# Gathering expert tokens before the last spectral tile: an early indirect gather, a one-hot product in PSUM, and transposes moved ahead

## The chip, the cores and the metric

The kernel runs on one core of a Trainium2 chip. The metric is the device time of one execution in microseconds (us). Before the change it is 496.32 us, the median of three runs (497.5, 496.32 and 492.94). Beside them stands one profiled execution of 498.16 us, whose span from first to last instruction is 496.4 us. All times of single instructions below come from that execution, and positions such as "at 401.55" are us from the start of its span.

## The reference, cut to what matters

Two blocks follow each other. The first filters each of 8 sequences (2496 positions, 256 channels) in the frequency domain. The second is a mixture of 8 experts: each token goes to the expert with the largest gate logit, each expert keeps the 80 tokens with the largest gate weight, and all other output rows are zero.

```python
X = np.fft.rfft(x, axis=1)
y = np.fft.irfft(X * (filt_r + 1j * filt_i)[None], n=2496, axis=1)   # (8, 2496, 256)
x = y.reshape(19968, 256)
logits = x @ w_gate
expert_idx = np.argmax(logits, axis=1)
gate_w = softmax(logits)[np.arange(N), expert_idx]
for e in range(8):
    tok_idx = np.where(expert_idx == e)[0]
    if len(tok_idx) > 80:
        tok_idx = the 80 of them with the largest gate_w
    h = np.maximum(x[tok_idx] @ w1[e], 0.0)            # w1[e]: 256 x 1024
    out[tok_idx] = gate_w[tok_idx, None] * (h @ w2[e])  # w2[e]: 1024 x 256
```

## The kernel before

Until about 300 us the kernel transforms all 8 sequences, writes their filtered spectra to DRAM (`yf`) and gets the gate logits directly from the spectra. Only then does it know which tokens are kept, and it transforms only those back. Kept tokens are grouped in 8 tiles of up to 128 tokens, one tile for each sequence.

**Choosing the tokens (`pick_...`, called from L871 on).** VectorE (DVE) and TensorE (PE) find the 80 best tokens of each expert. The last step, `pick_slots(2)` (L694), adds 16 small bf16 products in a PSUM tile called `misc` (L697), copies the result to `es` (L701) and derives from it three index tables: `idxg`, the row of `y_sel` that holds each token of each expert, `idxs`, its row in the output, and `idxt`, its row in the table of gate weights (`tokens`, L1048 to L1066). `es[:, 1]` is the tile of a token, `es[:, 0]` its place in the tile.

**Back transform of tile t.** `fetch(t)` (L467, a gather on the queue of GpSimd, POOL) brings rows of a table, `turn_rows(t, g)` (L483) transposes them on PE and ScalarE (ACT) copies them to SBUF, `add_rows(t, g)` (L493) adds 20 products of 128x256 in PSUM (L498). When a tile is complete, ACT copies it to `yr` (L502) and ACT's DMA queue writes it to `y_sel` in DRAM (L503). The order of the work on PE is the hand-written list `work` (L825 to L832), run piece by piece by `go`; the schedule is manual, so each engine executes in program order. Tiles come in order 0 to 7. On the way `spectrum(t)` (SyncE's queue, SP) loads spectra, and `weights(e, ...)` loads the 2 MB of each expert's weights on the SP queue: experts 0 and 1 after tile 4, 2 after tile 5, 3 to 5 when the buffers of the last spectra and table rows come free, 6 and 7 when experts 0 and 1 are done with theirs.

**Experts (class `Experts`, L995).** `gather(e)` (L1001) is an indirect DMA on the POOL queue which collects the 80 tokens of expert e from `y_sel`; since `y_sel` is read as a whole, it waits for the writes of all 8 tiles. `layer1(e)` (L1010) transposes the gathered rows on PE (L1015, 2 transposes), lets DVE copy them to `xs` (L1018), multiplies by w1 (L1022, 16 products of 128x80, which the profile lists as 32 records because an f32 product is two) and applies the ReLU, half on ACT (L1027), half on DVE (L1028). `layer2(e)` (L1032) multiplies by w2 (L1037, 8 products of 80x256), scales on ACT (L1040) and scatters 80 rows into the output through the POOL queue (L1042). The loop at L910 to L917 runs gather(e+3), layer1(e+1), layer2(e), after a first layer1(0) at L909. So each expert's transposes stand directly before its own products on PE.

Of the kernel before, what the change touches and what calls it, by code (L numbers as in the profile page):

```python
# [10 lines left out]
AL = mybir.AluOpType  # L11
AF = mybir.ActivationFunctionType
AX = mybir.AxisListType
F32 = mybir.dt.float32
BF16 = mybir.dt.bfloat16
# [8 lines left out]
B, S, C = 8, 2496, 256  # L24
# [57 lines left out]
def kernel(  # L82
# [95 lines left out]
    nc.gpsimd.memset(ones_bf[:], 1.0)  # L178


    NE, NY = 3, 2
    yf = {b: dpool.tile([128, NS, C], F32, name=f"yf_{b}") for b in range(B)}
    ypool = ctx.enter_context(tc.tile_pool(name="spec", bufs=NY))
    ysb = {}
# [48 lines left out]
    with ExitStack() as actx:  # L233
# [246 lines left out]
        def weights(e, p, tag):  # L480
            load_weights(e, p.tile([128, 2 * NFC * C], F32, name=f"w_{e}", tag=tag))
# [11 lines left out]
        def add_rows(t, g):  # L493
            if g == 0:
                pos[t] = yps.tile([128, 2, 512], F32, name=f"po_{t}", tag="y")
            for i in range(SG):
                s = SG * g + i
                nc.tensor.matmul(pos[t][:, 0, 0:C], lhsT=wts[t, g // 2][:, g % 2, i, :],  # L498
                                 rhs=ybs[t][:, s, :], start=(s == 0), stop=(s == NS - 1))
            if g == NS // SG - 1:  # L500
                yr = t2pool.tile([128, 2, C], F32, name=f"yr_{t}", tag="t2")
                nc.scalar.copy(out=yr[:, 0, :], in_=pos[t][:, 0, 0:C])  # L502
                nc.scalar.dma_start(out=y_sel[128 * t:128 * t + 128, :], in_=yr[:, 0, :])  # L503

        def pt(shape, dt, name, rnd):
# [168 lines left out]
        def pick_slots(part):  # L674
            f_t = st["f_t"]
            if part == 0:
                off_e = pt([128, 1], F32, "off_e", 1)
                nc.vector.tensor_copy(out=off_e[:], in_=st["poff"][:, 2, 0:1])
                slot = pt([128, KR], F32, "slot", 1)
                nc.vector.tensor_scalar(out=slot[:], in0=iota[:, 0:KR], scalar1=off_e[:, 0:1],  # L680
                                        scalar2=None, op0=AL.add)
                st["eplc"] = xpool.tile([128, KR, cap], BF16, name="eplc", tag="x")
                nc.vector.tensor_tensor(
                    out=st["eplc"][:], in0=slot[:].unsqueeze(2).to_broadcast([128, KR, cap]),
                    in1=iota[:, 0:cap].unsqueeze(1).to_broadcast([128, KR, cap]),
                    op=AL.is_equal)
            elif part == 1:
                st["eval"] = pt([128, KR, 4, E], BF16, "eval_", 1)
                for i in range(4):
                    nc.gpsimd.tensor_tensor(  # L690
                        out=st["eval"][:, :, i, :],
                        in0=f_t[:, i, :].unsqueeze(2).to_broadcast([128, KR, E]),
                        in1=ehot[:].unsqueeze(1).to_broadcast([128, KR, E]), op=AL.mult)
            else:  # L694
                pe = st["misc"][0:cap, 128:128 + 4 * E]
                for k in range(KR):
                    nc.tensor.matmul(pe, lhsT=st["eplc"][:, k, :],  # L697
                                     rhs=st["eval"][:, k].rearrange("p v e -> p (v e)"),
                                     start=(k == 0), stop=(k == KR - 1))
                es = pt([cap, 4, E], F32, "es", 1)  # L700
                nc.vector.tensor_copy(out=es[:].rearrange("p v e -> p (v e)"), in_=pe)  # L701
                nc.vector.scalar_tensor_tensor(out=idxg[:], in0=es[:, 1, :], scalar=128.0,
                                               in1=es[:, 0, :], op0=AL.mult, op1=AL.add)
                emp = pt([cap, E], F32, "emp", 1)
                nc.vector.tensor_scalar(out=emp[:], in0=es[:, 3, :], scalar1=st["off"][0:cap, 0:1],
                                        scalar2=float(N + S), op0=AL.is_le, op1=AL.mult)
                tokens(nc, sp, cap, es[:, 1, :], 0.0, es[:, 2, :], es[:, 3, :], -1.0, emp, idxs,
                       idxt)

        LATE, LEAD = 2, 2  # L710
        with tc.manual_schedule():
# [182 lines left out]
            for t in range(NE, 6):  # L894
                fetch(t)
            go(1)
            pick_slots(2)
            go(next(i for i, w in enumerate(work) if w[1] == NE))
            go(len(work))

            ex = Experts(nc, cap, ident, fp, lambda n: fps.tile([128, 512], F32, name=n, tag="f"),
                         lambda n: yps.tile([128, 2, 512], F32, name=n, tag="y"), y_sel[0:128 * B, :], out,
                         idxg, idxs, gate, w1s, w2s)
            for e in range(3):
                ex.gather(e)
            weights(3, st["yx"], "ys")
            weights(4, ypool, "ys")
            weights(5, t1pool, "t1")
            ex.layer1(0)  # L909
            for e in range(E):  # L910
                if e + 3 < E:
                    ex.gather(e + 3)
                if e + 1 < E:
                    ex.layer1(e + 1)
                ex.layer2(e)
                if e + 6 < E:
                    weights(e + 6, wpool, "w")  # L917

# [37 lines left out]
    with tc.If(n_bad > 0):  # L956
        with tc.tile_pool(name="spz", bufs=1) as mp:
            zc = mp.tile([128, C], F32, name="zc")
            nc.vector.memset(zc[:], 0.0)
            for t in range(B, B + NX):  # L960
                nc.sync.dma_start(out=y_sel[128 * t:128 * t + 128, :], in_=zc[:])
        select(tc, lg, cap, ident, ident_bf, iota, iota_i, pid, pid_i, lane, idxs, idxg, gate,
               idxb, more, nof, ohb)
        with (
            tc.tile_pool(name="xp2", bufs=1) as mp,
            tc.tile_pool(name="xps2", bufs=1, space=PSUM) as mps,
        ):
            for b in range(B):
                back(mp, mps, f"g{b}", lambda: spectrum_of(mp, b, f"g{b}"), 128 * b,
                     idxb[:, b:b + 1])  # L970
            for t in range(NX):
                ix = spill_lists(tc, mp, mps, t, cap, nof, ohb, iota, idxg)
                po = None
                for b in range(B):
                    po = back(mp, mps, f"x{t}_{b}", lambda: spectrum_of(mp, b, f"x{t}_{b}"),
                              128 * (B + t) if b == B - 1 else None, ix[:, b:b + 1],
                              start=(b == 0), stop=(b == B - 1), acc=po, pad=True)

        with (
            tc.tile_pool(name="w3", bufs=2) as wp3,  # L980
            tc.tile_pool(name="fp3", bufs=2) as fp3,
            tc.tile_pool(name="px3", bufs=2, space=PSUM) as px3,
            tc.tile_pool(name="ph3", bufs=2, space=PSUM) as ph3,
        ):
            ex = Experts(nc, cap, ident, fp3, lambda n: px3.tile([128, 512], F32, name=n, tag="f"),
                         lambda n: ph3.tile([128, 2, 512], F32, name=n, tag="y"), y_sel, out,
                         idxg, idxs, gate, w1s, w2s, "g")
            for e in range(E):
                load_weights(e, wp3.tile([128, 2 * NFC * C], F32, name=f"wg_{e}", tag="w"))
                ex.gather(e)  # L990
                ex.layer1(e)
                ex.layer2(e)


class Experts:  # L995
    def __init__(self, nc, cap, ident, fp, bank, banks, y_sel, out, idxg, idxs, gate, w1s, w2s,
                 nm=""):
        self.__dict__.update(locals())
        self.xg, self.hT = {}, {}

    def gather(self, e):  # L1001
        nc, cap = self.nc, self.cap
        xg = self.fp.tile([cap, C], F32, name=f"xg{self.nm}_{e}", tag="xg", bufs=4)
        nc.gpsimd.indirect_dma_start(
            out=xg[:], out_offset=None, in_=self.y_sel[:, :],
            in_offset=bass.IndirectOffsetOnAxis(ap=self.idxg[:, e:e + 1], axis=0),
            bounds_check=self.y_sel.shape[0] - 1, oob_is_err=False)
        self.xg[e] = xg

    def layer1(self, e):  # L1010
        nc, cap, nm = self.nc, self.cap, self.nm
        xg = self.xg.pop(e)
        px = self.bank(f"px{nm}_{e}").rearrange("p (k t) -> p k t", k=4)
        for k in range(NDB):
            nc.tensor.transpose(px[:, k, 0:cap], xg[:, 128 * k:128 * k + 128],  # L1015
                                self.ident[0:cap, 0:cap])
        xs = self.fp.tile([128, NDB, cap], F32, name=f"xs{nm}_{e}", tag="xs")
        nc.vector.tensor_copy(out=xs[:], in_=px[:, 0:NDB, 0:cap])  # L1018
        ph = self.banks(f"ph{nm}_{e}").rearrange("p i (j t) -> p i j t", j=4)
        for fc in range(NFC):  # L1020
            for k in range(NDB):
# [424 lines left out]
```

## Time and profile before

| what | us |
|---|---|
| median of the runs shown | 496.32 |
| profiled execution, its span | 498.16, 496.4 |
| PE busy in the span | 443.9 (89%) |
| last product of tile 7 ends | 401.55 |
| first transpose of expert 0 | 413.69 |
| last product of expert 7 ends | 484.83 |
| from there to the end of the span | 11.6 |

The numbers of single instructions are read from the timeline, where a row gives the start, the duration, the engine and line, the operation with the tile it writes and those it reads, the count of instructions merged in the row, and in brackets how long the engine was idle before it and what ended the wait. In the windows view a row gives, for one stretch of time, its length, the busy time and number of instructions of PE, PE's weight loads, DVE, ACT and POOL, then the granted clock of PE as a share of full speed, the busy share of the 16 DMA engines, and GB/s.

### The profile page before, as it was taken

The page shows a single profiled execution, that of the slowest core. Times are in us where ns is not written, and L with a number is a line of the kernel's source. Part 1 is how long each engine was busy: PE and PEld are TensorE (multiplying, and loading weights), DVE is VectorE, ACT ScalarE, POOL GpSimd, SP SyncE. Part 2 cuts the span into 40 slices and gives each one's busy share as a digit, 9 for nine tenths or more (in the row PEclk, how much of TensorE's full clock was granted, in tenths as well). Part 3 has the DMA queues.
Part 4 walks back from the last instruction along what each step waited for, and adds up shares of the span by engine and source line. Part 5 has one row for each costly group of instructions (what it writes and reads, how often), then busy time and mean ns, then how long its engine had stood idle before and what let it go on. Part 6 is the DMA issues. An engine that isn't in the chain of part 4 may idle for free. (4 is left out here: it accounts for less than half of the span.)

```text
span 496.4 us, 8607 instructions
## 1 busy us (share of the span) xinstructions
PE 443.9 (89%) x3363; PEld 416.1 (84%) x3363; DVE 201.1 (41%) x574; ACT 220.9 (45%) x339; POOL 176.4 (36%) x244
## 2 busy tenths in 40 slices
PE   5989999999999999999998889959999936999990
PEld 5879999999999999999997878848888825787870
DVE  2145544547844558644479973881000000001100
ACT  3846666666676667666664424312223300011110
POOL 7577343443444435444343471012340002031110
PEclk9989999999999999999999989999999975699997
DMA  7996467778778877889612239939999992073000
GB/s 228 275 296 204 146 192 255 238 254 270 246 249 247 275 258 235 264 246 393 257 46 101 113 108 368 403 130 394 352 365 396 381 391 89 0 272 108 21 16 11
DMA packets 38323, 112.82 MB, mean 227 GB/s; under 512 B 4386, under 2 KB 13922, under 8 KB 36482
## 3 DMA queue, kind: packets, MB, share of 16 engines
q1 hardware_dynamic: 27536, 75.36, 45.7%
q10 hardware_dynamic: 7330, 22.09, 11.3%
q0 software_dynamic: 3408, 14.74, 8.5%
q8 instruction: 29, 0.48, 0.4%
q14 instruction: 20, 0.16, 0.1%
HBM read 68.97 MB, written 43.20 MB: 226 GB/s over the span
## 5 line engine op out<-in xcount | busy, mean ns | idle before, releaser
L346 POOL TENSOR_TENSOR p<-p,p 128x256 f32<-128x256 f32 x160 | 114.5, 737 | 141.3 <-DVE p L340 98.7
L340 DVE TENSOR_TENSOR p<-pb,ft 128x512 f32<-128x512 f32 x160 | 102.3, 680 | 11.9 <-PE pb L332 6.7
L313 ACT COPY t<-pa 128x480 f32<-128x480 f32 x88 | 87.0, 1000 | 26.0 <-PE pa L307 25.7
L307 PE MATMUL pa<-wf_t,x 117*128 117x120 f32 x704 | 93.3, 281 | 5.7 <-DMA x<-in_x_dram 5.7
L307 PEld LDWEIGHTS pa<-wf_t,x 117*128 117x128 f32 x704 | 87.7, 198 | 5.7 <-DMA x<-in_x_dram 5.7
L355 PE MATMUL py<-gi,p 128*128 128x136 f32 x640 | 88.3, 281 | 1.6 <-POOL p L346 1.6
L332 PE MATMUL pb<-d_t,t 128*128 128x128 f32 x640 | 86.5, 279 | 2.1 <-remote 2.1
L355 PEld LDWEIGHTS py<-gi,p 128*128 128x128 f32 x640 | 80.2, 191 | 2.0 <-POOL p L346 2.0
L332 PEld LDWEIGHTS pb<-d_t,t 128*128 128x128 f32 x640 | 79.2, 194 | 2.6 <-remote 2.2
L323 ACT COPY t<-pt 128x512 f32<-128x512 f32 x80 | 46.8, 585 | 71.5 <-PE pt L321 66.3
L498 PE MATMUL po<-yb,wt 128*128 128x256 f32 x240 | 58.1, 387 | 1.3 <-ACT wt L491 1.3
L371 DVE COPY z<-py 128x16 f32<-128x16 f32 x80 | 14.8, 185 | 99.9 <-ACT ysp L367 65.9
L498 PEld LDWEIGHTS po<-yb,wt 128*128 128x128 f32 x240 | 44.4, 195 | 6.9 <-ACT wt L491 1.8
L321 PE MATMUL pt<-ident,t 128*128 128x128 f32 x320 | 49.0, 276 | 0.3 <-DVE p L340 0.3
L491 ACT COPY wt<-pw 128x512 f32<-128x512 f32 x40 | 23.2, 586 | 55.2 <-PE pw L487 50.7
L1022 PE MATMUL ph<-xs,w 128*128 128x80 f32 x256 | 37.0, 313 | 4.1 <-DVE xs L1018 3.0
L1022 PEld LDWEIGHTS ph<-xs,w 128*128 128x128 f32 x256 | 35.7, 227 | 5.5 <-DVE xs L1018 4.2
L1018 DVE COPY xs<-px 128x160 f32<-128x160 f32 x8 | 2.6, 324 | 91.4 <-PE px L1015 91.4
L367 ACT COPY ysp<-py 128x512 f32<-128x512 f32 x60 | 35.3, 588 | 8.9 <-PE py L355 8.9
L321 PEld LDWEIGHTS pt<-ident,t 128*128 128x128 f32 x320 | 38.4, 144 | 0.5 <-DVE p L340 0.5
L1037 PE MATMUL po<-w,hT 128*80 128x256 f32 x128 | 29.6, 387 | 0.0
L1042 POOL DMA_INDIRECT out_dram<-ys,idxs x8 | 7.5, 934 | 60.4 <-ACT ys L1040 60.4
(163 smaller groups left out, 329.4 us busy)
## 6 DMA issues: line engine op xcount, KB each, us to landing
out_dram<-zero_t SPq DMA_DIRECT2D x64, 312.0 KB
x<-in_x_dram SPq DMA_DIRECT2D x40, 468.0 KB
w<-in_moe_w_dram SPq DMA_DIRECT2D x16, 1024.0 KB
yf<-ysp ACTq DMA_DIRECT2D x30, 512.0 KB
yb<-yf SPq DMA_DIRECT2D x6, 2560.0 KB
yf<-ys ACTq DMA_DIRECT2D x10, 512.0 KB
x<-in_x_dram SPq DMA_DIRECT2D x8, 234.0 KB
d_t<-d_tbl SPq DMA_DIRECT2D x5, 256.0 KB
```

Of the source, the lines that this page charges most:

```text
L307: nc.tensor.matmul(out=ps[:, i, :, 2 * NS * cb:2 * NS * cb + 2 * NS], lhsT=xt[0:NJ * N1, (2 * k + i) % JC, 128 * cb:128 * cb + 128], rhs=w ...
L313: nc.scalar.copy(out=t1[:, 2 * k - h:2 * k - h + 2], in_=ps[:])
L321: nc.tensor.transpose(ps[:, i, cb, :], t1[:, a:a + 2, :].rearrange("p r n -> p (r n)"), ident[:])
L323: nc.scalar.copy(out=t2[:].rearrange("p i c -> p (i c)"), in_=ps[:].rearrange("p i c q -> p (i c q)"))
L332: nc.tensor.matmul(out=ps[:, cb, i], rhs=d_t[:, 2 * u + i, :], start=True, stop=True, lhsT=t2[:, i, 128 * cb:128 * cb + 128])
L340: nc.vector.tensor_tensor(out=pt, in0=ps[:].rearrange("p c s r q -> p (c s) r q"), in1=f.unsqueeze(2).to_broadcast([128, 2 * NDB, 2, NQ]), ...
L346: nc.gpsimd.tensor_tensor(out=yt[:, :, r, :], in0=yt[:, :, r, :], in1=pr[1][:, :, 1 - r, :], op=op)
L355: nc.tensor.matmul(out=ps[:, i, ZW * cb:ZW * cb + ZW], rhs=gi[:, cb, :], lhsT=yt[:, 2 * cb + i].rearrange("p r q -> p (r q)"), start=True, ...
L367: nc.scalar.copy(out=dst, in_=ps[:, :, E:E + C])
L498: nc.tensor.matmul(pos[t][:, 0, 0:C], lhsT=wts[t, g // 2][:, g % 2, i, :], rhs=ybs[t][:, s, :], start=(s == 0), stop=(s == NS - 1))
L1022: nc.tensor.matmul(ph[:, fc // 4, fc % 4, 0:cap], lhsT=self.w1s[e][:, k, 128 * fc:128 * fc + 128], rhs=xs[:, k, :], start=(k == 0), stop=( ...
L1037: nc.tensor.matmul(po[0:cap, :], lhsT=hT[:, fc, :], rhs=self.w2s[e][:, fc, :], start=(fc == 0), stop=(fc == NFC - 1))
```

## The change

- `Experts.gather` is split from the transposes. `gather(e, below)` with a limit reads only the rows of `y_sel` below it, and DVE first sets the destination to zero, so that tokens outside stay zero.
- For the first three experts (`NO = 3`) the gather is issued with the limit 896, that is, for tiles 0 to 6, at the place in the program that comes before the first product of tile 7. It waits for the writes of tiles 0 to 6 and for its zero fill.
- At the end of `pick_slots(2)` a one-hot matrix `last[p, e, i]` is made for these experts: 1 where token i of expert e is token p of tile 7. DVE computes `inl` (two small operations) and `diag` (a product of 80x240 in bf16), PE multiplies `diag` by ones (one bf16 product, 128x240), DVE compares with the partition number.
- `turn(e)` holds the transposes. For the first three experts each of the two transposes becomes a product with the identity, followed by a second product, of `yr` of tile 7 (still in SBUF) with `last`, which is added in PSUM. For the other experts it is the two transposes as before.
- The copy of tile 7 to `yr` is split: 128 columns by ACT, then 128 by DVE.
- The order on PE becomes turn(0), layer1(0), turn(1), layer1(1), turn(2), and then for each e: layer2(e), layer1(e+2), turn(e+3). Before it was, with the transposes inside, layer1(0), layer1(1), layer2(0), layer1(2), layer2(1) and so on. `xs` gets three buffers.
- The loads of the weights keep their order on the SP queue.

```diff
             if g == NS // SG - 1:
                 yr = t2pool.tile([128, 2, C], F32, name=f"yr_{t}", tag="t2")
-                nc.scalar.copy(out=yr[:, 0, :], in_=pos[t][:, 0, 0:C])
+                if t < B - 1:
+                    nc.scalar.copy(out=yr[:, 0, :], in_=pos[t][:, 0, 0:C])
+                else:
+                    nc.scalar.copy(out=yr[:, 0, 0:128], in_=pos[t][:, 0, 0:128])
+                    nc.vector.tensor_copy(out=yr[:, 0, 128:C], in_=pos[t][:, 0, 128:C])
+                st["yr"] = yr[:, 0, :]
                 nc.scalar.dma_start(out=y_sel[128 * t:128 * t + 128, :], in_=yr[:, 0, :])
...
                 tokens(nc, sp, cap, es[:, 1, :], 0.0, es[:, 2, :], es[:, 3, :], -1.0, emp, idxs,
                        idxt)
+                inl = pt([cap, NO], F32, "inl", 1)
+                nc.vector.tensor_scalar(out=inl[:], in0=es[:, 1, 0:NO], scalar1=float(B - 1),
+                                        scalar2=None, op0=AL.is_equal)
+                nc.vector.scalar_tensor_tensor(out=inl[:], in0=es[:, 0, 0:NO], scalar=1.0,
+                                               in1=inl[:], op0=AL.add, op1=AL.mult)
+                diag = fp.tile([cap, NO, cap], BF16, name="diag", bufs=1)
+                nc.vector.tensor_tensor(
+                    out=diag[:], in0=ident[0:cap, 0:cap].unsqueeze(1).to_broadcast([cap, NO, cap]),
+                    in1=inl[:].unsqueeze(2).to_broadcast([cap, NO, cap]), op=AL.mult)
+                last = st["last"] = fp.tile([128, NO, cap], F32, name="last", bufs=1)
+                pd = st["misc"][:, 192:192 + NO * cap]
+                nc.tensor.matmul(pd, lhsT=ones_bf[0:cap, :], start=True, stop=True,
+                                 rhs=diag[:].rearrange("p e t -> p (e t)"))
+                nc.vector.tensor_scalar(
+                    out=last[:].rearrange("p e t -> p (e t)"), in0=pd, scalar1=pid[:, 0:1],
+                    scalar2=1.0, op0=AL.subtract, op1=AL.is_equal)
...
             go(next(i for i, w in enumerate(work) if w[1] == NE))
+            go(next(i for i, w in enumerate(work) if w[:2] == ("m", B - 1)))
+            ex = Experts(...)
+            for e in range(NO):
+                ex.gather(e, 128 * (B - 1))
             go(len(work))
+            ex.extra = st["yr"], st["last"]
             for e in range(3):
-                ex.gather(e)
-            weights(3, st["yx"], "ys")
-            weights(4, ypool, "ys")
-            weights(5, t1pool, "t1")
-            ex.layer1(0)
+                ex.turn(e)
+                if e == 0:
+                    weights(3, st["yx"], "ys")
+                    weights(4, ypool, "ys")
+                    weights(5, t1pool, "t1")
+                if e < 2:
+                    ex.layer1(e)
             for e in range(E):
                 if e + 3 < E:
                     ex.gather(e + 3)
-                if e + 1 < E:
-                    ex.layer1(e + 1)
                 ex.layer2(e)
+                if e + 2 < E:
+                    ex.layer1(e + 2)
+                if e + 3 < E:
+                    ex.turn(e + 3)
                 if e + 6 < E:
                     weights(e + 6, wpool, "w")
...
+    def gather(self, e, below=None):
         nc, cap = self.nc, self.cap
         xg = self.fp.tile([cap, C], F32, name=f"xg{self.nm}_{e}", tag="xg", bufs=4)
+        if below is None:
+            below = self.y_sel.shape[0]
+        else:
+            nc.vector.memset(xg[:], 0.0)
+            self.part.add(e)
         nc.gpsimd.indirect_dma_start(
-            out=xg[:], out_offset=None, in_=self.y_sel[:, :],
+            out=xg[:], out_offset=None, in_=self.y_sel[0:below, :],
...
+    def turn(self, e):
+        xg = self.xg.pop(e)
         px = self.bank(f"px{nm}_{e}").rearrange("p (k t) -> p k t", k=4)
         for k in range(NDB):
-            nc.tensor.transpose(px[:, k, 0:cap], xg[:, 128 * k:128 * k + 128],
-                                self.ident[0:cap, 0:cap])
-        xs = self.fp.tile([128, NDB, cap], F32, name=f"xs{nm}_{e}", tag="xs")
+            x = xg[:, 128 * k:128 * k + 128]
+            if e not in self.part:
+                nc.tensor.transpose(px[:, k, 0:cap], x, self.ident[0:cap, 0:cap])
+                continue
+            yr, last = self.extra
+            nc.tensor.matmul(px[:, k, 0:cap], lhsT=x, rhs=self.ident[0:cap, 0:cap], start=True,
+                             stop=False)
+            nc.tensor.matmul(px[:, k, 0:cap], lhsT=yr[:, 128 * k:128 * k + 128],
+                             rhs=last[:, e, :], start=False, stop=True)
+        xs = self.fp.tile([128, NDB, cap], F32, name=f"xs{nm}_{e}", tag="xs", bufs=3)
         nc.vector.tensor_copy(out=xs[:], in_=px[:, 0:NDB, 0:cap])
+        self.xs[e] = xs
+
+    def layer1(self, e):
+        xs = self.xs.pop(e)
         ph = self.banks(f"ph{nm}_{e}").rearrange("p i (j t) -> p i j t", j=4)
```

More of the change, by code (lines that the diff above doesn't have):

```diff
@@ L178 @@
     nc.gpsimd.memset(ones_bf[:], 1.0)
-    NE, NY = 3, 2
+    NE, NY, NO = 3, 2, 3
     yf = {b: dpool.tile([128, NS, C], F32, name=f"yf_{b}") for b in range(B)}
@@ L898 @@
             go(next(i for i, w in enumerate(work) if w[1] == NE))
+            go(next(i for i, w in enumerate(work) if w[:2] == ("m", B - 1)))
+            ex = Experts(nc, cap, ident, fp, lambda n: fps.tile([128, 512], F32, name=n, tag="f"),
+                         lambda n: yps.tile([128, 2, 512], F32, name=n, tag="y"),
+                         y_sel[0:128 * B, :], out, idxg, idxs, gate, w1s, w2s)
+            for e in range(NO):
+                ex.gather(e, 128 * (B - 1))
             go(len(work))
-            ex = Experts(nc, cap, ident, fp, lambda n: fps.tile([128, 512], F32, name=n, tag="f"),
-                         lambda n: yps.tile([128, 2, 512], F32, name=n, tag="y"), y_sel[0:128 * B, :], out,
-                         idxg, idxs, gate, w1s, w2s)
+            ex.extra = st["yr"], st["last"]
             for e in range(3):
-                ex.gather(e)
-            weights(3, st["yx"], "ys")
-            weights(4, ypool, "ys")
-            weights(5, t1pool, "t1")
-            ex.layer1(0)
+                ex.turn(e)
[5 more added lines that the diff above has]
+                    ex.layer1(e)
             for e in range(E):
@@ L990 @@
                 ex.gather(e)
+                ex.turn(e)
                 ex.layer1(e)
@@ L998, in __init__ @@
         self.__dict__.update(locals())
-        self.xg, self.hT = {}, {}
-    def gather(self, e):
+        self.xg, self.xs, self.hT = {}, {}, {}
+        self.part, self.extra = set(), None
+    def gather(self, e, below=None):
         nc, cap = self.nc, self.cap
         xg = self.fp.tile([cap, C], F32, name=f"xg{self.nm}_{e}", tag="xg", bufs=4)
+        if below is None:
[3 more added lines that the diff above has]
+            self.part.add(e)
         nc.gpsimd.indirect_dma_start(
-            out=xg[:], out_offset=None, in_=self.y_sel[:, :],
+            out=xg[:], out_offset=None, in_=self.y_sel[0:below, :],
             in_offset=bass.IndirectOffsetOnAxis(ap=self.idxg[:, e:e + 1], axis=0),
-            bounds_check=self.y_sel.shape[0] - 1, oob_is_err=False)
+            bounds_check=below - 1, oob_is_err=False)
         self.xg[e] = xg
-    def layer1(self, e):
+    def turn(self, e):
         nc, cap, nm = self.nc, self.cap, self.nm
@@ L1014, in layer1 @@
         for k in range(NDB):
-            nc.tensor.transpose(px[:, k, 0:cap], xg[:, 128 * k:128 * k + 128],
-                                self.ident[0:cap, 0:cap])
-        xs = self.fp.tile([128, NDB, cap], F32, name=f"xs{nm}_{e}", tag="xs")
+            x = xg[:, 128 * k:128 * k + 128]
[8 more added lines that the diff above has]
+        xs = self.fp.tile([128, NDB, cap], F32, name=f"xs{nm}_{e}", tag="xs", bufs=3)
         nc.vector.tensor_copy(out=xs[:], in_=px[:, 0:NDB, 0:cap])
+        self.xs[e] = xs
+    def layer1(self, e):
+        nc, cap, nm = self.nc, self.cap, self.nm
+        xs = self.xs.pop(e)
         ph = self.banks(f"ph{nm}_{e}").rearrange("p i (j t) -> p i j t", j=4)
```

## The prediction

> **What bounds the kernel now.** I read the page's slices first. PE is busy nearly everywhere, with one hole, and the granted clock sags right behind it:
>
> ```profile
> PE   5989999999999999999998889959999936999990
> PEclk9989999999999999999999989999999975699997
> ```
>
> The hole is slice 33 (each is 12.4 us), between the last tile and the first expert. The timeline there:
>
> ```profile
> 397.93 3.62 PE L498 MATMUL po<-yb,wt 128*128 128x256 f32 x16
> ...
> 401.99 0.33 ACTq L503 DMA_DIRECT2D y_sel<-yr  x1
> 408.88 0.94 POOL L1004 DMA_INDIRECT xg<-y_sel,idxg  x1 [36.90 <-DMA w<-in_moe_w_dram]
> ...
> 413.69 0.50 PE L1015 MATMUL px<-ident,xg 80*128 80x80 f32 x2 [12.14 <-issue]
> 414.66 7.11 PE L1022 MATMUL ph<-xs,w 128*128 128x80 f32 x32 [0.47 <-DVE xs L1018]
> 435.06 3.80 PE L1022 MATMUL ph<-xs,w 128*128 128x80 f32 x32 [0.42 <-DVE xs L1018]
> ```
>
> The reader is to see two things. PE stands 12.1 us while tile 7 goes to DRAM and back: 0.8 to the end of the issue at 402.32, 6.56 until the gather starts, 0.94 for the gather's issue, 3.84 for its landing. And the same 32 records take 7.11 us before 431 and 3.80 after. The windows view, cut on a grid of 3.41 us, says why:
>
> ```profile
> 25.56:28.97 3.41, 1.34 (x13) 1.19 (x12) 1.85 (x3) 0.50 (x2) 1.86 (x3) 1.00 0.95 299
> 284.97:288.38 3.41, 1.48 (x20) 1.36 (x20) 3.38 (x7) 0.58 (x1) 1.52 (x3) 1.00 0.02 5
> 325.94:329.35 3.41, 1.59 (x8) 1.43 (x8) 2.81 (x23) 0.00 (x0) 0.34 (x1) 1.00 0.00 0
> 401.02:404.43 3.41, 0.53 (x3) 0.12 (x1) 0.00 (x0) 0.37 (x1) 0.00 (x0) 1.00 1.03 397
> 424.91:428.32 3.41, 3.41 (x17) 3.41 (x17) 0.00 (x0) 0.00 (x0) 0.00 (x0) 0.50 0.00 0
> 428.32:431.73 3.41, 3.41 (x14) 2.74 (x13) 0.49 (x1) 0.44 (x1) 0.00 (x0) 0.50 0.00 0
> ```
>
> Every change of the granted clock in this trace falls on that grid (28.97, 32.38, 288.38, 291.79, 332.76, 336.17, 404.43, 431.73). A window with 1.34 or 1.48 us of PE work is followed by half clock, one with 1.59 is not. And half clock lasts as long as PE sees only layer1's 80-column products, though it is 100% busy with them (424.91 to 428.32); it ends with the window in which layer2's 256-column products begin. At full clock the same 80-column stream keeps it full. From 434.34 on PE is full-speed and bound by itself.
>
> **The hole, changed.** Tile 6 is issued to DRAM at 391.60, 10.39 us before tile 7's 401.99. Its packets are the only ones of ACT's queue in 395.5 to 397.5, tile 7's in 405.6 to 407.6, both 3.3 to 5.6 us after the issue's end among 100% busy DMA engines:
>
> ```profile
> q10 hardware_dynamic: 144, 0.13, 19.0%
> ...
> q10 hardware_dynamic: 143, 0.13, 18.8%
> ```
>
> So tile 6's write frees its gather as tile 7's did, 6.56 us after the issue ends: 391.93 + 6.56 = 398.5. With 0.95 issue and 3.84 landing, expert 0 has its rows at 403.3; I add 0.35, since before the weights' traffic ran out while this gather landed and now it does not: 403.65. The hole becomes 2.1 us (401.55 to 403.65). Bounds: not below 0.75, for tile 7 must still pass through the two half copies (0.27 and 0.2 by the 0.37 of the 256-column row, one after the other because DVE's waits for ACT's, and hops); not above 12.1, if the rows arrive only when the weights have drained. I take 2.1 by the nearest rows. Gathers of experts 1 and 2 follow 1.25 and 2.5 us later on POOL, needed 10 and 20 us later. POOL's next gather (expert 3) still waits for tile 7's write, with only scatter(0) behind it, which is not ready before.
>
> **The clock behind the hole.** A window that contains the whole 2.1 us has at most 1.3 us of PE work, below 1.48. The grid is free of the kernel's start. With s us of the window before 401.55, it stays full only for s from about 1.5 to 2.7 of 3.41, and 80-column work after the hole counts for less, so I give full clock three chances in ten. The Trainium skill ("TensorE: Matmul & The Clock Gate", Part 1 and "HAM oscillation") has the same 3.4 us window, but warns only of gaps over about 3.4 us, and says full speed returns after about 3.4 us of sustained work. By that rule the 2.1 us hole is harmless, or costs at most 1.7 us, and the sum below is about 481. Here a 2.07 us wait (before 28.42) halved the clock, and after 413.7 it took 18 us of unbroken work to return; I follow the rows.
>
> **The experts' PE time.** Full-clock pieces from 435 to 485: layer1 3.64, layer2 3.45, two transposes 0.30, wait for `xs` 0.42, together the 7.81 by which layer1 rows follow each other.
> - turn(3) to (7) and layer1(2) lose the wait: 6 x 0.42 = 2.5 gained, hidden behind layer2. The gathers feeding them are issued about 2 us after layer2(e-1) and needed 11 us after it; if they came later PE would wait.
> - turn(0), (1), (2): four two-record products, 8 records, instead of two. At half clock 0.222 each (7.11/32) = 1.78; at full 0.114 = 0.91.
>
> Half clock, from the first product of turn(0): 2.4 (1.78 and the 0.6 to `xs`), layer1(0) 6.95, turn(1) and wait 2.25, layer1(1) 6.9, turn(2) 1.8, layer2(0) 4.2 (2.7 us at half clock, 1.0 to 4.4 by where the grid falls; 1.7 before): 24.5. The rest at full clock: 7 x 3.45 + 6 x 3.64 + 5 x 0.30 + 0.2 = 47.7. With the hole 74.3, against 484.83 - 401.55 = 83.3: **9.0 gained**. At full clock the 24.5 is 14.25: 19.2 gained.
>
> **What the one-hot matrix costs, earlier.** Its PE product stands in program order between L697 and the next transposes, and waits for DVE:
>
> ```profile
> 336.52 0.75 PE L697 MATMUL misc<-eval__1_3628,eplc 128*80 128x32 bf16 x16
> 337.13 0.64 PE L487 MATMUL pw<-ident,gts 128*128 128x128 f32 x4
> 337.39 0.19 DVE L701 COPY es<-misc 80x32 f32<-80x32 f32 x1 [2.29 <-PE misc L697]
> 339.31 0.16 DVE L1066 TENSOR_TENSOR idxs<-tk_l,tk_s 80x8 int32<-80x8 f32 x1
> ```
>
> `inl` comes after `idxs` in DVE's order: to 339.47, then 0.35 for two small ones, 0.35 for `diag` (240 of the 1280 elements that took 1.49, and start): PE gets on at 340.3 instead of 337.13, **3.2 us late**. All tile work is queued behind it; from 337.10 to 401.55 PE is busy 63.12 of 64.45 us, so nearly nothing absorbs it (0.4 for the 0.75 us wait for table rows at 367). A 3.2 us hole also halves the clock here: 1.0 on average (0 to 1.7, half of one window). Together **+3.8**, from 2.4 to 5.
>
> At nothing: three zero fills and `last` on DVE, which has no instruction from 339.5 to 414; the gather and weight queues, which keep their order. If DVE were busy, the zero fills (0.3 us each) would delay the gathers.
>
> **Sum.** -9.0 + 3.8 = -5.2: 498.16 becomes 493.0. The profiled execution is 1.84 above the median of the runs, so 491.1; a further 0.4 because its layer2(0) had only 1.7 us at half clock where 2.7 is the average: **490.7**.
>
> **Rivals.**
> - *The clock stays full.* For it: at s in the right part of the window, or if the hole is near 0.75. Against: 1.34 and 1.48 were not enough. -19.2 + 3.8 = -15.4: 480.9.
> - *The gather is starved by weights* (slower). Weights of experts 4 and 5 fill the DMA engines until 412.2; tile 7's write saw no packet for 3.3 us. If the gather's rows land only as they drain, PE starts as late as before, and loses the 3.8 of the one-hot stall and 1.0 of longer transposes at half clock: +4.8, 501. It decides from a hole of 7.3 us on (11.1 - 7.3 = 3.8). Against: tile 7's write did get through, 5 us before the drain, and the old gather's 0.13 MB moved in 411.2 to 412.2 beside 0.11 MB of weights.
> - *Half clock, with a longer hole* (3 to 5 us) or a longer stall: 492 to 496, no change that shows.
>
> That the gather still waits for tile 7 is excluded: in program order it stands before that write.
>
> **Chances.** Half clock as summed 0.62 (490.7, give or take 2.2), full clock 0.28, starved or worse 0.07, unknown 0.03. About 1% is what a measurement of this kernel can tell, so the lines are 491.4 and 501.3. Of the half-clock case 0.38 lies below the first, 0.24 above. Faster 0.66, same 0.26, slower 0.08. The range takes in the full-clock case (from 478.5) and the half-clock case with its bounds (to 496).
>
> **What would show it.** First L1056 product about 2 us after the last L498 product; layer1(0) and (1) near 7 us each (half clock) or 3.7 (full); a PE hole of 3 us behind the sixteen bf16 products of the pick; no wait before layer1(2) to (7). It is wrong if the hole is over 7 us, if PE loses no time at the pick, or if half clock ends inside layer1.

## The result, and the profile after

In 20 executions of each kernel on one chip the median went from 496.39 us (492.94 to 499.58) to **492.62 us** (489.67 to 499.03): ratio 0.992, 95% interval 0.990 to 0.994. The profiled execution after took 492.98 us, its span is 491.1. All ratios here leave out executions more than 1.5% above the fastest of the same kernel on that chip, while medians take them in, so a ratio can differ from the quotient of its medians; of e11 below three of six are left out, the profiled one with them. The slices of the page, PE's busy tenths and its granted clock:

```profile
PE   5889999999999999999998989977999997999990
PEclk9999999999999999999999979976999995599996
```

The slice with a 3 is gone; the low clock behind it is still there (two slices of 5, where before it was 7, 5 and 6). The timeline of the changed kernel where tile 7 ends and the experts begin (start, duration, engine and line, what it does, count, and in brackets the wait before it):

```profile
400.64 3.62 PE L498 MATMUL po<-yb,wt 128*128 128x256 f32 x16
...
401.91 0.94 POOL L1040 DMA_INDIRECT xg<-y_sel,idxg  x1 [26.75 <-ACT wt L491]
...
407.89 0.69 PE L1056 MATMUL px<-ident,xg 80*128 80x80 f32 x2 [3.62 <-DMA xg<-y_sel,idxg]
...
410.27 7.12 PE L1070 MATMUL ph<-xs,w 128*128 128x80 f32 x32 [0.42 <-DVE xs L1061]
...
419.51 7.12 PE L1070 MATMUL ph<-xs,w 128*128 128x80 f32 x32 [0.42 <-DVE xs L1061]
...
428.12 5.09 PE L1085 MATMUL po<-w,hT 128*80 128x256 f32 x16
...
433.05 3.69 PE L1070 MATMUL ph<-xs,w 128*128 128x80 f32 x32
```

The hole is 3.6 us instead of 12.1. The gather is issued 2.35 us before tile 7 ends, but its rows land 5.0 us after the issue (402.85 to 407.89). layer1(0) and layer1(1) take 7.12 us each, layer1(2) 3.69 with no wait before it. The windows view shows the hole and what follows it (length; busy time of PE, weight loads, DVE, ACT, POOL; granted clock; DMA share; GB/s):

```profile
403.80:407.21 3.41, 0.46 (x3) 0.06 (x1) 0.29 (x1) 0.27 (x1) 1.26 (x2) 1.00 1.05 382
407.21:410.62 3.41, 2.32 (x10) 2.13 (x10) 0.33 (x1) 0.00 (x0) 0.00 (x0) 0.50 1.09 370
```

PE works 0.46 us in the first window and has half clock from the second on. The DMA engines are full throughout (1.05, 1.09). The timeline of the other place, at the pick:

```profile
335.62 0.76 PE L702 MATMUL misc<-eval__1_3628,eplc 128*80 128x32 bf16 x16
...
338.87 0.41 DVE L720 TENSOR_TENSOR diag<-ident,inl 80x240 bf16<-80x240 f32 x1
339.32 0.36 PE L725 MATMUL misc<-diag,ones_bf 80*128 80x240 bf16 x1 [2.95 <-DVE diag L720]
339.48 1.06 PE L487 MATMUL pw<-ident,gts 128*128 128x128 f32 x4
```

PE waits 2.95 us for `diag`; the next transposes start 3.86 us after the sixteen bf16 products do, before it was 0.61. So the time moved like this between the two profiled executions:

| stretch | before | after | change |
|---|---|---|---|
| start to the sixteen products of the pick | 336.52 | 335.62 | -0.90 |
| from there to the next transposes | 0.61 | 3.86 | +3.25 |
| from there to the end of tile 7 | 64.42 | 64.78 | +0.36 |
| hole | 12.14 | 3.63 | -8.51 |
| first expert product to the end of layer2(7) | 71.14 | 71.40 | +0.26 |
| the rest, with what lies around the span | 13.33 | 13.69 | +0.36 |

Together -5.18 (498.16 to 492.98). The first row is chance: the change touches nothing before the pick. The row that wants explaining is the last but one: the new order takes waits away from the experts, and yet their time did not shrink. Up to layer1(2) they take 25.16 us instead of 21.37, 3.8 more, since the three turns have four times the records and lie with more of layer2(0) in the half clock (layer2(0) took 5.09 us, at full clock it takes 3.62); from there on 46.24 instead of 49.77, 3.5 less.

### The profile page after: what moved, and what is told of

It is laid out like the page before. It is cut to its first block, busy times and chain, and to the rows that moved or that the text cites. A ratio compares the mean times of both kernels' runs of the same rounds, so it can differ in the third digit from the quotient of the medians.

```text
span 491.1 us, 8653 instructions
## 1 busy us (share of the span) xinstructions
PE 451.3 (92%) x3382; PEld 423.1 (86%) x3382; DVE 202.7 (41%) x582; ACT 221.7 (45%) x339; POOL 176.4 (36%) x244
## 5 line engine op out<-in xcount | busy, mean ns | idle before, releaser
L355 PE MATMUL py<-gi,p 128*128 128x136 f32 x640 | 89.3, 283 | 1.6 <-POOL p L346 1.6
L498 PE MATMUL po<-yb,wt 128*128 128x256 f32 x240 | 59.3, 393 | 0.6 <-ACT wt L491 0.6
L487 PEld LDWEIGHTS pw<-ident,gts 128*128 128x128 f32 x160 | 20.4, 145 | 8.0 <-issue 3.7
```

What stands on the lines that cost most here:

```text
L355: nc.tensor.matmul(out=ps[:, i, ZW * cb:ZW * cb + ZW], rhs=gi[:, cb, :], lhsT=yt[:, 2 * cb + i].rearrange("p r q -> p (r q)"), start=True, ...
```

## The experiments

Theory: the change has three separate effects, a shorter hole, a new order, and a stall at the pick, and most of its worth is lost because the clock falls behind the hole and does not come back during 80-column products. Rivals: the clock has nothing to do with the hole; the pick's stall is absorbed; the gather's latency is its own rather than caused by the weights beside it. The runs were made on several chips, so they are compared by "ratio", which is to the kernel before on the same chip, whose median there was 500.49 (first four), 500.15 (next four), 497.39 (next three) and 500.16 (last).

| run | us | ratio (95%) |
|---|---|---|
| e1_warm: after + 8 filling products | 485.67 | 0.9733 (0.9667 to 0.9799) |
| e2_late: after, one-hot product later | 492.46 | 0.9867 (0.9805 to 0.9929) |
| e3_before_warm: before + 26 filling products | 498.11 | 0.9948 (0.9903 to 0.9993) |
| e6_order: before + new order only | 496.84 | 0.995 (0.9917 to 0.9983) |
| e0_after: the changed kernel | 494.95 | 0.991 (0.9877 to 0.9942) |
| e4_warm_late: e1 and e2 together | 479.53 | 0.9597 (0.9555 to 0.9638) |
| e5_gate: after, weights 3 to 5 held back | 481.88 | 0.9649 (0.9596 to 0.9701) |
| e7_before_full: before + 31 filling products | 493.05 | 0.987 (0.9815 to 0.9926) |
| e8_gate_late: e5 and e2 together | **473.29** | **0.9516 (0.9488 to 0.9543)** |
| e9_before_gate: before, weights 3 to 5 held back | 490.54 | 0.9864 (0.9825 to 0.9902) |
| e10_onehot: e6 + the one-hot product, unused | 498.48 | 1.0024 (0.9994 to 1.0055) |
| e11_gate_hold_order: e6, weights held, 14 filling products | 485.20 | 0.9627 (0.9572 to 0.9682) |

**The changed kernel again.** 

> The changed kernel itself, beside the experiments on one chip. Expected ratio to the kernel before 0.992 (0.989 to 0.995), about 496.5 us where the kernel before stands at 500.5; the variant with eight filling products gained 10.9 us over it by this (485.7), and the one with the late one-hot product 4 us (492.5). If the late variant's gain is not real, the changed kernel stands at 492 to 493 here and the one-hot product's place costs nothing.

It came at 0.991. In its profiled execution the hole was 2.44 us, with the same half clock behind it (410.22 to 430.7): the window in which most of the hole falls has 1.53 us of PE work.

```profile
401.97 0.95 POOL L1040 DMA_INDIRECT xg<-y_sel,idxg  x1 [25.27 <-DMA w<-in_moe_w_dram]
...
408.27 0.42 PE L1056 MATMUL px<-ident,xg 80*128 80x80 f32 x2 [2.44 <-DMA xg<-y_sel,idxg]
```

```profile
403.40:406.81 3.41, 2.43 (x12) 1.79 (x10) 0.29 (x1) 0.27 (x1) 1.72 (x2) 1.00 1.09 373
406.81:410.22 3.41, 1.53 (x12) 1.41 (x13) 0.32 (x1) 0.00 (x0) 0.00 (x0) 1.00 1.05 334
410.22:413.63 3.41, 3.41 (x19) 3.41 (x18) 0.00 (x0) 0.00 (x0) 0.00 (x0) 0.50 1.07 394
```

**Is it the clock?** e1 adds products that nothing reads between tile 7 and turn(0), each with the shape of the tiles' own:

```diff
+        def hold(n):
+            ps = fps.tile([128, 512], F32, name="hold", tag="f")
+            for i in range(n):
+                nc.tensor.matmul(ps[:, 0:C], lhsT=ident[:], rhs=ybs[B - 1][:, i % NS, :],
+                                 start=True, stop=True)
...
             go(len(work))
+            hold(8)
             ex.extra = st["yr"], st["last"]
```

> The changed kernel with 8 filler products (128x256, f32, result unused) on TensorE between the last product of tile 7 and turn(0); they take about 3.5 us and fit the 3.6 us hole. Clock theory (the hole costs most by halving the granted clock): the hole's end stays, layer1(0) and layer1(1) take 3.7 us instead of 7.1, time near 481.7 (492.6 - 10.9). Rival (the start of the experts is slow for another reason, such as its 80-column products or fresh weights): layer1 stays at 7.1 us, time stays at 492.6.

The timeline of e1:

```profile
406.17 3.62 PE L734 MATMUL hold<-yb,ident 128*128 128x256 f32 x16
...
409.75 0.42 PE L1063 MATMUL px<-ident,xg 80*128 80x80 f32 x2
...
411.25 3.80 PE L1077 MATMUL ph<-xs,w 128*128 128x80 f32 x32 [0.42 <-DVE xs L1068]
...
416.38 3.80 PE L1077 MATMUL ph<-xs,w 128*128 128x80 f32 x32 [0.44 <-DVE xs L1068]
```

The first expert product comes 3.4 us after tile 7's end (406.34), as in the kernel without the fill; only the hole is full. layer1 now takes 3.80, and the clock is full from 344.5 to 474.2. The time is 0.018 of the ratio lower than e0, some 9 us. So behind tile 7 it is the clock, not the wait for the rows, that costs most after the change.

The same on the kernel before, with its hole of 12 us (26 of them at the same place), went less well.

```diff
             go(len(work))
+            hold(26)
```

> The kernel before with 26 of the filler products between tile 7 and layer1(0), about 11.4 us in its hole of 12.1. Clock theory: the 20 us at half clock after the hole shrink by 8.8, time near 487.6, so better than the changed kernel without moving any gather. Rival: no change (496.4), or slower if the fillers delay something.

The ten executions lie in two groups, 494.7 to 496.5 and 499.7 to 502.8, and the profiled one, 500.7, shows why: the fill ended 1.56 us before the rows were there, and the clock fell at 420.6, at the end of the window in which the last 0.6 us of that rest and the 0.5 us wait for `xs` lie. e7 differs only in its `hold(31)`.

> The kernel before with 31 filling products instead of 26, so that they reach past the gather's landing (11.4 us of them ended 1.56 us before the first expert product last time, and the clock fell some 3 us later). Theory (what cost the clock was that rest; with no rest over 0.5 us the clock stays full through the first two experts, whose products then take 3.7 us for each half layer instead of 7.1): 8 to 10 us less than the kernel before, ratio 0.980 to 0.984, with the hole left as long as it was. Rival (products of 80 columns cannot hold the full clock by themselves on cold weights): layer1 at 7.1 us again, ratio 0.993 to 1.0.

It came at 0.987, with layer1 at 3.80 and 3.77 and no half clock from 339 to 482. The gain is smaller than expected; of the difference the profile shows that its hole, 13.2 us, was 1.1 longer than in the profiled kernel before. The windows of layer1's products alone, on each run's own grid of clock windows (length; PE busy, weight loads busy, clock, DMA share, GB/s). In e3:

```profile
417.17:420.58 3.41, 2.01 (x18) 2.01 (x19) 1.00 0.16 53
420.58:423.99 3.41, 3.29 (x16) 3.07 (x15) 0.50 0.00 0
```

The same view of e7:

```profile
417.53:420.94 3.41, 3.11 (x28) 2.96 (x27) 1.00 0.01 2
420.94:424.35 3.41, 2.33 (x21) 2.37 (x22) 1.00 0.00 0
```

And of e11 (told of below), whose clock fell at 417.51:

```profile
410.69:414.10 3.41, 2.52 (x22) 2.52 (x23) 1.00 0.24 75
414.10:417.51 3.41, 2.03 (x19) 1.91 (x18) 1.00 0.06 7
```

A window with 2.01 or 2.03 us of layer1's products is followed by half clock, one with 2.33 is not. That is no bound on busy time, though. With all of PE's work, the two transposes too, e3's window holds as much as e7's (2.33, all of it layer1):

```profile
417.17:420.58 3.41, 2.34 (x20) 2.21 (x21) 0.32 (x1) 0.00 (x0) 0.00 (x0) 1.00 0.16 53
```

Nor do the prediction's 1.48 (falls) and 1.59 (holds) bound it: the first is 136-column f32 and 6-column bf16 products, the second the tiles' 256-column ones. The changed kernel, long before its experts, loses the clock after a window with more than either:

```profile
280.92:284.33 3.41, 1.74 (x13) 1.32 (x13) 3.38 (x6) 1.08 (x2) 1.85 (x2) 1.00 0.38 156
284.33:287.74 3.41, 2.46 (x26) 2.30 (x25) 3.38 (x8) 0.59 (x1) 1.86 (x2) 0.50 0.02 5
```

In the same stage, with a somewhat different mix of products, e7 keeps it after 1.73 us (284.40 to 287.81). So busy time alone does not decide. At half clock the shape matters: behind a window full of 80-column products the clock stays halved (the prediction's 424.91 to 428.32), behind one with 1.4 us (e9) or more of layer2's 256-column products it is full again, behind one with 0.9 (e6) or 1.1 (e11) not yet. That the number of columns in a window is what counts would fit much of this, but it is argued, not shown.

**The new order alone.** e6 leaves out the early gather and the one-hot product, and keeps turns and layers in the new order.

```diff
-            for e in range(NO):
-                ex.gather(e, 128 * (B - 1))
             go(len(work))
-            ex.extra = st["yr"], st["last"]
+            for e in range(NO):
+                ex.gather(e)
```

> The changed kernel without its early part: all gathers after tile 7's write as before, no one-hot matrix, no second product, tile 7's copy on ACT alone; only the order turn(e+3) after layer1(e+2) is kept. Theory: hole 12.1 and half clock as before, but no 0.42 us wait before layer1(2) to (7): 2.5 us under before, 493.9. Rival (the order gains nothing, all of the change's gain is the gather): 496.4.

0.995, which is 2.5 us (0.9 to 4.2), as expected.

**The one-hot product at the pick.** e10 is e6 with `inl`, `diag`, the product and the compare left in at the pick; against e6:

```diff
+                inl = pt([cap, NO], F32, "inl", 1)
...
+                nc.tensor.matmul(pd, lhsT=ones_bf[0:cap, :], start=True, stop=True,
+                                 rhs=diag[:].rearrange("p e t -> p (e t)"))
...
```

> The changed order of turns with the gathers after tile 7 as in the kernel before, and the one-hot product at the pick kept, though nothing reads its result: beside the order alone (ratio 0.995) it shows what the product at the pick costs. Prediction's step: 3.8 us (2.4 to 5), ratio 1.0002 to 1.005. Rival (free, absorbed by the tiles' own waits): ratio 0.994 to 0.996. If the stall also costs a further stretch of half clock: ratio above 1.005.

1.0024 against e6's 0.995: 3.7 us, as predicted, and the intervals do not meet. The stall, in e10's timeline:

```profile
336.00 0.26 PE L721 MATMUL misc<-diag,ones_bf 80*128 80x240 bf16 x1 [3.08 <-DVE diag L716]
```

e2 is the opposite: the changed kernel with that product and the compare moved to just before tile 7's first product.

```diff
-                nc.tensor.matmul(pd, lhsT=ones_bf[0:cap, :], start=True, stop=True,
-                                 rhs=diag[:].rearrange("p e t -> p (e t)"))
...
+                def mark_last():
+                    nc.tensor.matmul(pd, lhsT=ones_bf[0:cap, :], start=True, stop=True,
+                                     rhs=diag[:].rearrange("p e t -> p (e t)"))
...
+                st["mark_last"] = mark_last
...
                 ex.gather(e, 128 * (B - 1))
+            st["mark_last"]()
             go(len(work))
```

> The changed kernel with the bf16 product of the one-hot matrix and the comparison after it moved from the end of the pick to just before the first product of tile 7; DVE's inl and diag stay where they are. Theory (the wait of 2.95 us and the half clock after it push all tiles later): tiles end 3.1 to 4.6 us earlier, time near 488.5. Rival (the tiles are paced by the DMA queues, so the stall is absorbed by tile 7): time stays at 492.6 within 0.7.

0.9867 against e0's 0.991 is 2.1 us, less than expected, and the intervals overlap, so alone it settles nothing. With the clock held, in e4 (e1's and e2's lines together), it is clearer:

> Both repairs at once: the one-hot product and the compare after it moved from the pick to just before the first product of tile 7, and eight filling products (128x256, f32, nothing reads them) between tile 7 and the first expert. Theory (two separate losses, the idle PE at the pick and the half clock behind the hole): they add, so 2.5 to 4 us below the variant with the filling products alone, 481.5 to 483.5 us where that one stood at 485.7. Rival (the pick's stall is absorbed by what follows it, as the tiles wait for later transfers anyway): 485 to 487, no gain over the filling products alone.

0.9597 against e1's 0.9733, and (below) e8's 0.9516 against e5's 0.9649: both pairs apart. The four pairs give 3.7, 2.1, 6.8 and 6.6 us; weighted by their intervals, as if these were independent, 4.6 us (3.1 to 6.0). Part of it is clock. In the profiled executions the five with the product at the pick (after, e0, e1, e5, e10) have a stretch of half clock, 3.4 or 6.8 us long, which begins in the stall or at most 1.1 us behind it; none of the nine without it has one there. An earlier stretch, of 3.4 to 10.2 us, is in all fourteen and over when the sixteen products of the pick are.

**Whose latency is the gather's?** e5 is the changed kernel with the weights of experts 3 to 5 held back on SP's queue, behind a transfer of 64 bytes that needs the first expert's hidden layer.

```diff
                 ex.turn(e)
-                if e == 0:
-                    weights(3, st["yx"], "ys")
-                    weights(4, ypool, "ys")
-                    weights(5, t1pool, "t1")
                 if e < 2:
                     ex.layer1(e)
+                if e == 0:
+                    nc.sync.dma_start(out=hold_d[:, :], in_=ex.hT[0][0:1, 0, 0:16])
+                    weights(3, st["yx"], "ys")
+                    weights(4, ypool, "ys")
+                    weights(5, t1pool, "t1")
```

> The changed kernel, with the weights of experts 3 to 5 held back on SP's queue by a small transfer that waits for the first expert's hidden layer, so that no weight moves while tile 7's rows and the three gathers land. Theory (the hole of 3.6 us is the gather's landing of 5.0 us, lengthened by the weights' traffic; unloaded it lands in about 2.5 to 3.5 us): the hole shrinks to 1 to 2.2 us, the half clock stays, so 1.4 to 2.6 us less than the changed kernel. Rival (the latency is the gather's own): hole 3.3 to 3.8 and the time unchanged. Second rival: with a rest under 1.5 us the window holds enough work, the clock stays full, and the gain is some 10 us. Third: weights 3 to 5 come late and the fourth expert waits, 2 to 6 us lost.

The timeline of e5:

```profile
401.87 0.94 POOL L1042 DMA_INDIRECT xg<-y_sel,idxg  x1 [26.31 <-DMA w<-in_moe_w_dram]
...
402.11 3.62 PE L499 MATMUL po<-yb,wt 128*128 128x256 f32 x16
...
405.56 0.35 PE L1058 MATMUL px<-ident,xg 80*128 80x80 f32 x2
...
406.08 0.45 PE L1060 MATMUL px<-last,yr 128*128 128x80 f32 x2 [0.17 <-ACT yr L506]
...
407.39 3.80 PE L1072 MATMUL ph<-xs,w 128*128 128x80 f32 x32 [0.42 <-DVE xs L1063]
...
408.85 0.95 POOL L1042 DMA_INDIRECT xg<-y_sel,idxg  x1 [3.54 <-DMA y_sel<-yr]
```

The gather is issued at the same distance from tile 7's end as in e0 (3.86 us), but its rows are there before the tile ends (PE loads them as weights at 405.35, 2.54 us after the issue ends), where they took 5.35 us after the issue in e0. There is no hole; what is left is 0.17 us for the half copy of `yr`. The clock stays full with no fill, and layer1(2) to (7) follow without a wait, so the held weights are not late. It is the second rival of the expectation, and 0.026 of the ratio, 13 us, below e0.

e9 does the same to the kernel before, with nothing of the change.

```diff
+            ex.layer1(0)
+            nc.sync.dma_start(out=hold_d[:, :], in_=ex.hT[0][0:1, 0, 0:16])
             weights(3, st["yx"], "ys")
             weights(4, ypool, "ys")
             weights(5, t1pool, "t1")
-            ex.layer1(0)
```

> The kernel before with nothing of the change, only the weights of experts 3 to 5 held behind the first hidden layer. Theory (in the hole of 12 us some 7 us is tile 7's write waiting for its packets' turn behind queued weights, and the gather's landing is lengthened by them too; unloaded they take 2.5 us each): the hole falls to 6.3 to 7.5 us, the half clock stays as the hole is longer than a clock window, 4.5 to 6 us less than before, ratio 0.988 to 0.991: as much as the whole change without its one-hot product. Rival (write and gather have these latencies by themselves): hole 11 to 12.5, ratio 0.998 to 1.002. Second rival: weights come late for the fourth expert, ratio over 1.0.

The timeline of e9:

```profile
400.72 0.33 ACTq L504 DMA_DIRECT2D y_sel<-yr  x1
403.46 0.94 POOL L1006 DMA_INDIRECT xg<-y_sel,idxg  x1 [28.35 <-issue]
...
406.11 0.50 PE L1017 MATMUL px<-ident,xg 80*128 80x80 f32 x2 [5.83 <-issue]
407.08 7.12 PE L1024 MATMUL ph<-xs,w 128*128 128x80 f32 x32 [0.47 <-DVE xs L1020]
```

From the end of the write's issue to the start of the gather's is 2.4 us instead of 6.56, the landing 1.7 instead of 3.84, the hole 5.8 instead of 12.1. The clock still falls. This alone gains 6.8 us (ratio 0.9864), a little more than expected and at least as much as the whole change (0.991 or 0.992, intervals that overlap with this one), without any of its work. The traces do not show whether the weights delay the small transfers by their place in a queue or by the bandwidth that they take.

**The best version.** e8 has the change, the held weights (e5's lines) and the later one-hot product (e2's).

> The weights of experts 3 to 5 held behind the first hidden layer (481.9 us alone, ratio 0.965) and the one-hot product moved from the pick to just before tile 7's first product. Theory (the pick's stall of 2.95 us and the half-clock stretches beside it are a loss of their own): 3 to 6 us less than the held weights alone, ratio 0.953 to 0.959. Rival (the tiles make the stall good later): ratio 0.963 to 0.967.

The timeline of e8, at the pick and where the experts begin:

```profile
333.04 0.75 PE L703 MATMUL misc<-eval__1_3629,eplc 128*80 128x32 bf16 x16
...
333.64 0.63 PE L488 MATMUL pw<-ident,gts 128*128 128x128 f32 x4
...
397.83 0.34 PE L1062 MATMUL px<-ident,xg 80*128 80x80 f32 x2
...
399.66 3.80 PE L1076 MATMUL ph<-xs,w 128*128 128x80 f32 x32 [0.42 <-DVE xs L1067]
```

473.29 us against 497.39, faster than either kernel and than every other run here. No stall at the pick, no hole, and no half clock from 329 to 462. What the early gather itself is worth then, e11 asks: the order alone, weights held, the hole that is left filled; against e6, beside e5's lines:

```diff
             go(len(work))
+            hold(14)
             for e in range(NO):
                 ex.gather(e)
```

> What is left for the early gather and the one-hot product once the clock is held by other means: the changed order of turns, the gathers after tile 7 as in the kernel before, no one-hot product, the weights of experts 3 to 5 held behind the first hidden layer, and fourteen filling products over the hole that is left (5.8 us in the kernel before with the weights held). Theory (the effects add: held weights 6.8 us, order 2.5, full clock through the first two experts 9.6): 18.9 us less than before, ratio 0.959 to 0.967; the early gather with its late one-hot product (ratio 0.952) is then worth some 5 us by itself. Rival (as with 26 fillers in the kernel before, the clock falls after all): ratio 0.978 to 0.985.

0.9627 against e8's 0.9516 makes the early gather with its late one-hot product worth some 5.5 us (2.5 to 8.6, from both intervals). But the ratio rests on three executions (478.01, 482.88 and 484.95). All six spread from 478.01 to 488.65, and their median is 0.970 of the kernel before, which would make it 9 us. The longest is the profiled one, in which the clock fell behind the window with 2.03 us of layer1 work shown above (a wait of 1.24 us between layer1(0) and layer1(1) lay in it). So the fill does not make that version safe, and what the early gather is worth with the clock held in every execution stays open.

## Why the prediction was right, and where not

- **The sum for the profiled execution was 493.0, and it came at 492.98.** That close it is luck, because errors cancel: the hole 1.5 longer and the first two experts 0.7 longer than summed, the end 0.4; the later experts 1.5 and the pick with the tiles 0.2 shorter, and 0.9 before the pick that has nothing to do with the change. The time predicted from it, 490.7, is 1.9 below the median, and the term that was off is the step from profile to median: the profiled execution of before stood 1.8 above its median and 0.4 more was taken off for its layer2(0), but the profiled execution after stands only 0.4 above its own.
- **The hole, 2.1.** It was 3.6 in one execution and 2.4 in another. The gather's start was placed well (3.05 us before tile 7's end; 2.35 and 3.86), its landing too short: 3.84 + 0.35 from a gather at which the weights' traffic was running out, where under full traffic it is 5.0 and 5.35, and without the weights at most 2.54 (e5). So the weights do lengthen the landing, as the starved rival had it, but far from its point of decision, 7.3 us.
- **The clock falls behind the hole and 80-column products don't bring it back.** Right: half clock from 407.2 to 431.1 in the changed kernel, 25.2 us from the first expert product to layer1(2) where 24.5 was summed, and e1 shows that a filled hole is enough to keep it. The working behind the 0.28 for full clock was not sound: it took 1.48 and 1.59 us as a bound, and they are different products. In e0 tile 7 filled 2.43 us of its window, within the 1.5 to 2.7 that was to keep the clock (for a hole of 2.1), and it fell one window later, after 1.53 us. The full-clock case was in none of the 32 executions: the lowest is 489.67. Its size was about right: 480.9 predicted, 0.969 of before; e5 reached 0.965, with the hole at zero. The rule of the Trainium skill that was weighed ("TensorE: Matmul & The Clock Gate", "HAM oscillation" and Part 1: gaps over about 3.4 us, full speed after some 3.4 us of work) would have given 481 for a hole of 2.1 us. The hole came at 3.6 us in one trace, over that gap, but one of 2.44 us halved the clock too (e0), and it stayed halved for 23.9 and 20.5 us of nearly unbroken work. Here the measurement stands against the rule.
- **The order, 2.5.** e6: 2.5. In the trace the experts at full clock follow each other by 7.13 us (433.05 to 440.18) instead of 7.81: 0.68 each, not 0.42, as the two transposes too hide between the products. This accounts for the 1.5 us by which the experts' rest (47.7 summed) came shorter, 46.2, and it balanced the longer hole.
- **The one-hot product, +3.8.** e10 against e6: 3.7; all four pairs: 4.6 (3.1 to 6.0). The transposes started 3.25 us later than before, where 3.2 was summed from `diag` and its two small operations. The half clock was put at 1.0, at most 1.7 for one window; the stretch behind the stall is one window long in three of the five traces and two in the others, so 1.0 may be too small, but the pairs do not settle it.
- **At nothing:** zero fills and `last` run on an otherwise idle DVE and nothing waits for them; SP's weights were not late even when held (no wait before layer1(2) to (7) in e5).
- **Why the gain is small:** the hole gave 8.5 us and the order 3.5, while the longer work at half clock took 3.8 back and the pick 3 to 5. The first two experts still pay some 9 us for the clock (e1), and 2.4 to 3.6 us of hole remained to cause it. With 4.6 for the pick and 3.6 for the hole that is 17 us, most of the 20 by which e8 (0.9516) lies below the changed kernel (0.991).

## What to carry to other kernels

When a wait shrinks from 12 us to 3, ask whether what is left still trips the clock: here the last 3 us cost 9 more, and were removed not by more early work but by holding bulk weight loads off their queue while a small write and a small gather were on the path. A small product that waits for VectorE in the middle of TensorE's program should be put where its input has long been ready: moving it gave some 5 us (3.1 to 6.0).

## What was not expected of the hardware

- Holding three experts' weights back by one 64-byte transfer shortened the time from the issue of a 128 KB write to the start of its reader from 6.56 to 2.4 us, and a gather's landing from 3.84 to 1.7 us (e9). Before, the DMA engines' share beside the write was 1.0.
- Busy time alone is not what the clock follows. It fell after a window with 2.34 us of PE work (e3) and held after one with 2.33 (e7); it fell after 1.74 (the changed kernel) and held after 1.73 (e7) and after 1.59 (the kernel before).
- Filling products cost no time of their own where PE would have waited (in e1 the first expert product came 3.4 us behind tile 7, without them 3.6), but 1.56 us of rest after 11.4 us of them (e3) went with a fallen clock in the profiled execution, and five of the ten times lie some 5 us above the other five.
